# Float64 words turned into float32 through a PSUM bank, in a fused attention and two-layer expert kernel

## The chip, the cores and the metric

One NeuronCore of a Trainium2 chip (trn2) runs the whole program in one launch. The metric is the device time of one execution in microseconds (us), from the first to the last instruction and what lies around them; the median of three runs stands for the kernel.

## The reference, cut to what matters

Three layers follow each other on 1536 tokens (2 sequences of 768) of 384 channels.

```python
def reference(...):
    # 1: linear attention with a decaying state, 8 heads of 48
    state = w * state + k_t v_t ;  y_t = r_t (state + (u * k_t) v_t)
    # 2: dense layer, d_ff = 2048
    h = x @ w_in
    g = np.maximum(h, 0.0) + alpha * np.minimum(h, 0.0)
    x = g @ w_out
    # 3: each token goes to one of 8 experts (argmax of x @ w_gate), at most 384 tokens each
    y = np.maximum(x @ w1[e], 0.0) @ w2[e]
    out = softmax weight of e * y
```

Two inputs, `w_in` (384x2048) and `w_out` (2048x384), come as float64 (a float32 draw times a double). The kernel reads them as pairs of 32-bit words and makes float32 out of them itself.

## The kernel before

The dense layer is computed in 3 blocks of 512 tokens (`SIZES`), each in 16 slices of 128 hidden units; slice g is unit group g % 16 of block g // 16. A slice (`moe1_slice`, L603) does, in the order in which its instructions stand in each engine's queue: the steps of `work[g][5]`; the first product on TensorE (L599, 9 matmuls of 512 columns, since each factor is split into a high and a low float32r part and three of the four products are taken); on ScalarE the leak (L615); `work[g][0]`; on VectorE the second half of the leak (L618); on ScalarE the high part `gh` (L619); `work[g][1]`; on VectorE the low part `gl` (L622); `work[g][2]` and `work[g][3]`; the second product of slice g-2 on TensorE (L584); `work[g][4]`. Every engine takes its queue in order, so a step that waits holds all that stands behind it on its engine. The first product of slice g writes one of two banks (`ps_h`), so it waits for `gl` of slice g-2.

The second product of a block (`moe1_second`, L575) has four accumulators of 128 tokens x 384 channels, one PSUM bank each (`ps_acc`, four banks): per slice 4 x 3 matmuls of 384 columns, with the activations as the stationary operand and `w_out` as the moving one.

Attention runs ahead of the dense layer: tiles 0 to 3 before slice 0, tiles 4 to 7 in the slices of block 0, tiles 8 to 11 in those of block 1, in steps that `PHASES` (L314) puts into the slots: `turn` (TensorE transposes L182, L194; then VectorE L188 writes `rT`, ScalarE L202 `kT`, GpSimd a bonus), `score0` (TensorE L209, VectorE L212 writes `A`), `score1`, `output` (TensorE L218, L225, L236; VectorE L228 and the state), `finish` (TensorE L261; ScalarE L269, VectorE L270). Their PSUM tiles come in turn from two banks (`ps_a`).

The weights of the dense layer come in 8 pieces (q = 0 to 7, two slices each), and each piece in two parts (0: of `w_in`, 1: of `w_out`) of 128x768 numbers. `convert_moe1` (L339) turns one part into float32 and splits it. With `f` a scratch tile in SBUF (`spare`), `low` and `high` the two words of each number, its steps are `m0` (ScalarE L355, f from high), `s0` (VectorE L358, on f alone), `s1` (VectorE L361, f from low and f), `s2` (VectorE L364, low from high and f) and `s3` (ScalarE L367 the high part, GpSimd L368 the low part, each 128x768). Two parts are done before slice 0 (q = 0 and 1, part 0); the other 14 are spread over block 0 by `CONVERT` (L993): a step's number p, counted from slice `at`, means slice p // 5 and slot (5, 0, 1, 2, 4)[p % 5]. The two parts of a piece have different scratch halves for q < 4.

After a block its four accumulators are copied to SBUF (`evac` in `routing_steps`, L423) as rows; each 128 rows are turned for the gate product (`logit`, L428, then `logit_mm`, L437); the rows are scattered to `disp` in DRAM by expert. The experts follow; ahead of them one early block of expert 0 is computed (`Early`), and `keep_warm` (L752) fills TensorE with 6 matmuls (`warm_e`) while the rows of expert 0 are read back.

Of the kernel before, what the change touches and what calls it, by code (L numbers as in the profile page):

```python
# [18 lines left out]
P = 128  # L19
# [4 lines left out]
def kernel(  # L24
# [16 lines left out]
    nc = tc.nc  # L41
# [6 lines left out]
    DC = DM // P  # L48
# [269 lines left out]
    def rows_of(blk):  # L318
        return p1.tile([P, max(SIZES), ROW], F32, tag="rows", name=f"rows{blk}")
# [9 lines left out]
    def load_moe1(q, parts=(0, 1)):  # L329
        if 0 in parts:  # L330
            t = wpool.tile([P, 4 * DC * EF], I32, tag="w", name=f"rm{q}")
            raws[q] = (t[:, 0:2 * DC * EF], t[:, 2 * DC * EF:])
            nc.sync.dma_start(raws[q][0].rearrange("p (c n) -> p c n", c=DC),
                              moe_w_in[:, q * EF:(q + 1) * EF].bitcast(I32).rearrange("(c p) n -> p c n", p=P))
        if 1 in parts:
            nc.sync.dma_start(raws[q][1].rearrange("p (c n) -> p c n", c=2),
                              moe_w_out[q * EF:(q + 1) * EF, :].bitcast(I32).rearrange("(c p) n -> p c n", p=P))

    def convert_moe1(q, part, eng):  # L339

        n = DC * EF
        raw = raws[q][part].rearrange("p (n t) -> p n t", t=2)
        if part == 0:
            wsl[q] = wpool.tile([P, 4 * n], F32R, tag="w", name=f"wm{q}")
            if q in LOAD_AT:
                load_moe1(LOAD_AT[q])
        hi = wsl[q][:, part * 2 * n:part * 2 * n + n]
        lo = wsl[q][:, part * 2 * n + n:part * 2 * n + 2 * n]
        low, high = raw[:, :, 0], raw[:, :, 1]
        at = part * n if 2 * q < 8 else 0  # L350
        f = spare[:, at:at + n].bitcast(I32)

        def m0():

            nc.scalar.activation(f.bitcast(F32), high.bitcast(F32), AF.Copy, scale=2.0 ** -112)  # L355

        def s0():
            nc.vector.tensor_scalar(f, f, 3, 0x7FFFFFF8, op0=ALU.logical_shift_left, op1=ALU.bitwise_and)  # L358

        def s1():  # L360
            nc.vector.scalar_tensor_tensor(f, low, 29, f, op0=ALU.logical_shift_right, op1=ALU.bitwise_or)  # L361

        def s2():
            nc.vector.scalar_tensor_tensor(low, high, -0x80000000, f, op0=ALU.bitwise_and, op1=ALU.bitwise_or)  # L364

        def s3():
            nc.scalar.copy(hi, low.bitcast(F32))  # L367
            eng.tensor_tensor(lo, low.bitcast(F32), hi.bitcast(F32), ALU.subtract)  # L368

        return [m0, lambda: None, s0, s1, s2, s3]  # L370
# [44 lines left out]
    def routing_steps(blk, R, s0, SUB, before=()):  # L415
# [4 lines left out]

        end = blk == NBLK - 1

        def evac(s):  # L423
            def f():
                nc.scalar.copy(R[:, s0 + s, 0:DM], accs[(blk, s0 + s)])
            return f

        def logit(s):  # L428
            pt = bank(f"px2_{nm}_{s}", "acc" if end else "att")
            for c in range(DC):  # L430
                nc.tensor.transpose(pt[:, c * P:(c + 1) * P], R[:, s0 + s, c * P:(c + 1) * P], ident)
            pool, tag = ((p1, "x2T"), (p2, "cv"), (p2, "cv"), (p1, "x2T"))[s0 + s if end else 0]
            T[s] = pool.tile([P, DC, P], F32, tag=tag, name=f"x2T{nm}_{s}")
            src = pt[:, 0:DM].rearrange("p (c t) -> p c t", c=DC)
            return lambda: (nc.vector.tensor_copy if end and s0 + s < 2 else nc.scalar.copy)(T[s], src)

        def logit_mm(s):  # L437
            if s == 0 and end:
                T["pl"] = bank(f"pl{nm}")
                T["lg"] = T["pl"][:, 0:SUB * E].rearrange("p (s e) -> p s e", s=SUB)  # L440
            elif s == 0:
                T["lg"] = p2.tile([P, SUB, E], F32, tag="lg", name=f"lg{nm}")
            pl = T["pl"][:, s * E:(s + 1) * E] if end else bank(f"pl{nm}_{s}")[:, 0:E]
            for c in range(DC):
                for x in range(2):
                    nc.tensor.matmul(pl[64 * x:64 * x + 64], T[s][:, c, 64 * x:64 * x + 64], wg[:, c, :],
                                     start=(c == 0), stop=(c == DC - 1), skip_group_check=True)
            return (lambda: None) if end else lambda: nc.vector.tensor_copy(T["lg"][:, s, :], pl)

# [102 lines left out]
        def pair(s):  # L552
            def f(now=True):
                then = []
                if s > 0:
                    then.append(logit_mm(s - 1))
                if s < SUB:
                    then.append(logit(s))
                if now:
                    for t in then:  # L560
                        t()
                return then
            return f

        T["logit"], T["logit_mm"] = logit, logit_mm
        ev = [evac(s) for s in range(SUB)]
        T.update(choose=choose, weigh=weigh, count=count, place=place, scatter=scatter, total=total)
        steps = [pair(s) for s in range(SUB + 1)] + [lambda: weave(choose()), settle]
        return ev, steps, T
# [285 lines left out]
    with tc.manual_schedule():  # L855
# [134 lines left out]
        c1[5]()  # L990


        CONVERT = {0: (0, 0, 0, 0, 2, 3), 1: (-5, 1, 1, 1, 5, 9), 2: (-4, -2, -1, 2, 3, 7), 4: (-1, 0, 2, 5, 6, 7), 5: (-4, -1, 0, 1, 4, 6), 3: (-4, 0, 2, 5, 5, 7), 6: (-3, -1, 2, 4, 5, 7), 7: (-6, -6, -4, -2, 2, 4)}  # L993
        OTHERS = (-1, -1, 0, 0, 0, 5)
        work = [([], [], [], [], [], []) for _ in range(NBLK * NFT)]
        for q in range(NW):
            for x in range(2):
                if (q, x) in ((0, 0), (1, 0)):
                    continue
                at = 2 * q - 3 if x == 0 else 2 * q  # L1000
                c = []

                def step(n, c=c, q=q, x=x):
                    if n == 0:
                        c.extend(convert_moe1(q, x, nc.gpsimd))
                    c[n]()
                for n, p in enumerate(CONVERT.get(at, OTHERS)):
                    g = at + p // 5
                    work[g][(5, 0, 1, 2, 4)[p % 5]].append(lambda n=n, step=step: step(n))
# [147 lines left out]
```

## Time and profile before

| | |
|---|---|
| median of 3 runs | 466.55 us (466.14 to 466.82) |
| profiled execution | 466.23 us, span 464.5 us |
| busy: TensorE matmul / VectorE / ScalarE / GpSimd | 437.4 / 271.0 / 208.2 / 157.7 us |
| mean granted TensorE clock | 0.989 of full speed |

The span runs from the first to the last instruction; 1.7 us lie around it. Busy shares are averages over the whole program, and block 0 (about 36 to 133 us), in which the weights are converted, looks different from the rest; so the views below cut the time into stretches.

### The profile page before, as it was taken

The numbers are of one execution on the slowest core, as the hardware profiler recorded it, in microseconds if no ns is written. First come the engines' busy times: TensorE is split into PE (matmuls) and PEld (weight loads), VectorE is DVE, ScalarE is ACT, GpSimd is POOL, SyncE is SP. The second block draws the span as 40 slices with busy tenths as digits, with TensorE's granted clock in tenths as the row PEclk, the third lists the DMA queues.
The fourth block names the chain that finished last, engine by engine and source line by source line (L and its number), as shares of the span: only waits on it lengthen the run. The fifth ranks groups of instructions, "written<-read, shape, count | busy, mean of one in ns | idle before, by whom it ended". The sixth has DMA issues, their size and how long they took to land. (4 is left out here: it accounts for less than half of the span.)

```text
span 464.5 us, 7861 instructions
## 1 busy us (share of the span) xinstructions
PE 437.4 (94%) x3039; PEld 385.1 (83%) x3039; DVE 271.0 (58%) x470; ACT 208.2 (45%) x344; POOL 157.7 (34%) x138
## 2 busy tenths in 40 slices
PE   7977799699899999999999999999999999999995
PEld 6766699588788988989988888987988889898884
DVE  6998998999753444445333665354463535452651
ACT  1236634354344333323244444336473646553761
POOL 6855457464440231100300030033343515241660
PEclk9999979989999999999999999999999999999999
DMA  6999950649610207101700020018956556580200
GB/s 129 229 281 250 318 157 4 183 158 361 172 30 15 52 2 233 57 0 43 299 1 1 0 87 0 1 56 290 382 178 239 188 169 212 172 271 35 72 10 25
DMA packets 70605, 62.28 MB, mean 134 GB/s; under 512 B 41935, under 2 KB 58239, under 8 KB 70561
## 3 DMA queue, kind: packets, MB, share of 16 engines
q1 hardware_dynamic: 68832, 57.29, 41.1%
q0 software_dynamic: 1728, 4.40, 2.5%
q8 instruction: 28, 0.46, 0.4%
q14 instruction: 17, 0.13, 0.1%
HBM read 49.99 MB, written 12.62 MB: 135 GB/s over the span
## 5 line engine op out<-in xcount | busy, mean ns | idle before, releaser
L584 PE MATMUL acc<-wm,gh 128*128 128x384 f32 x384 | 102.0, 347 | 0.5 <-POOL wm L368 0.5
L599 PE MATMUL h<-xh,wm 128*128 128x512 f32 (+1 forms) x294 | 86.2, 402 | 4.4 <-DVE gl L622 4.4
L618 DVE SCALAR_TENSOR_TENSOR h<-ng,sign,h 128x512 f32<-128x512 f32 x48 | 36.1, 752 | 68.2 <-ACT ng L615 68.2
L584 PEld LDWEIGHTS acc<-wm,gh 128*128 128x128 f32 x384 | 69.9, 191 | 4.7 <-POOL wm L368 0.8
L775 PE MATMUL eh<-we,d 128*128 128x512 f32 x252 | 65.1, 403 | 4.5 <-PEq L847 3.2
L584 PE MATMUL acc<-wm,gl 128*128 128x384 f32 x192 | 65.4, 341 | 0.0
L599 PEld LDWEIGHTS h<-xh,wm 128*128 128x128 f32 x294 | 52.6, 190 | 14.2 <-issue 2.8
L615 ACT ACTIVATE ng<-h,slope 128x512 f32<-128x512 f32 x48 | 33.1, 689 | 60.1 <-PE h L599 60.0
L775 PEld LDWEIGHTS eh<-we,d 128*128 128x128 f32 x252 | 45.7, 188 | 15.5 <-issue 4.4
L619 ACT CAST gh<-h 128x512 fp32r<-128x512 f32 x48 | 28.1, 586 | 60.8 <-DVE h L618 60.8
L674 ACT CAST we<-re 128x768 fp32r<-128x768 f32 x64 | 50.6, 839 | 9.6 <-DMA re<-in_moe_w_dram 6.8
L677 POOL TENSOR_TENSOR we<-re,we 128x768 fp32r<-128x768 f32 x21 | 40.6, 1932 | 38.5 <-ACT we L674 32.2
L790 DVE TENSOR_TENSOR hl<-pht,hh 128x512 fp32r<-128x512 f32 x28 | 19.4, 692 | 51.6 <-ACT hh L789 49.8
L368 POOL TENSOR_TENSOR wm<-rm,wm 128x768 fp32r<-128x768 f32 x16 | 32.2, 2013 | 47.4 <-ACT wm L367 43.6
L799 PE MATMUL ey<-we,hh 128*128 128x384 f32 x224 | 48.1, 346 | 0.0
L677 DVE TENSOR_TENSOR we<-re,we 128x768 fp32r<-128x768 f32 x43 | 40.3, 965 | 11.9 <-ACT we L674 8.9
L522 POOL DMA_INDIRECT disp<-rows,sl x12 | 12.6, 1051 | 99.9 <-DVE run L543 64.4
L599 PE MATMUL h<-xl,wm 128*128 128x512 f32 (+1 forms) x147 | 42.1, 395 | 0.1
L622 DVE TENSOR_TENSOR gl<-h,gh 128x512 fp32r<-128x512 f32 x48 | 33.0, 687 | 15.6 <-ACT gh L619 15.6
L799 PEld LDWEIGHTS ey<-we,hh 128*128 128x128 f32 x224 | 37.8, 189 | 0.3 <-ACT hh L789 0.3
L584 PEld LDWEIGHTS acc<-wm,gl 128*128 128x128 f32 x192 | 36.6, 191 | 0.0
L599 PEld LDWEIGHTS h<-xl,wm 128*128 128x128 f32 x147 | 27.7, 191 | 7.0 <-DVE xl L270 0.3
(181 smaller groups left out, 618.8 us busy)
## 6 DMA issues: line engine op xcount, KB each, us to landing
re<-in_moe_w_dram SPq DMA_DIRECT2D x32, 768.0 KB, 7.2
rm<-in_moe_w_in_dram SPq DMA_DIRECT2D x8, 768.0 KB, 8.1
rm<-in_moe_w_out_dram SPq DMA_DIRECT2D x8, 768.0 KB, 7.5
disp<-rowss SPq DMA_DIRECT2D x1, 4825.0 KB, 16.0
drow<-disp SPq DMA_DIRECT2D x7, 579.0 KB, 3.9
out_dram<-rowss SPq DMA_DIRECT2D x1, 2304.0 KB, 22.4
kn<-in_k_dram SPq DMA_DIRECT2D x10, 192.0 KB, 4.6
rn<-in_r_dram SPq DMA_DIRECT2D x10, 192.0 KB, 4.8
```

Of the source, the lines that this page charges most:

```text
L368: eng.tensor_tensor(lo, low.bitcast(F32), hi.bitcast(F32), ALU.subtract)
L584: nc.tensor.matmul(accs[(blk, s)], gs[g][a][:, s * P:(s + 1) * P], wout[b][:, ft % 2, :], start=(ft == 0 and n == 0), stop=(ft == NFT - 1 ...
L599: nc.tensor.matmul(phs[g][:, cols[0]:cols[1]], win[a][:, c, o:o + P], xs[b][:, c, cols[0]:cols[1]], start=(n == 0), stop=(n == 3 * DC - 1))
L615: nc.scalar.activation(ng, ph, AF.Relu, scale=slope[:, ft:ft + 1])
L618: nc.vector.scalar_tensor_tensor(ph, ng, sign[:, ft:ft + 1], ph, op0=ALU.mult, op1=ALU.add)
L619: nc.scalar.copy(gh, ph)
L622: nc.vector.tensor_tensor(gl, ph, gh.bitcast(F32), ALU.subtract)
L674: nc.scalar.copy(t[:, sl], src[:, sl])
L677: le.tensor_tensor(t[:, sl2], src[:, sl], t[:, sl].bitcast(F32), ALU.subtract)
L775: nc.tensor.matmul(ph[q], d[x][:, c, :], ww[y][:, c, :], start=(n == 0), stop=(n == 3 * DC - 1))
L790: nc.vector.tensor_tensor(hl, pt, hh.bitcast(F32), ALU.subtract)
L799: nc.tensor.matmul(py, hT[q][x][:, c * P:(c + 1) * P], ww[y][:, c, :], start=(q == 0 and not low and c == 0 and y == 0), stop=(q == 1 and ...
```

## The change

- In block 0 (`TURNED`) the second product is summed transposed: the weights are the stationary operand, the activations the moving one, in three accumulators of 128 channels x 512 tokens, so 3 x 3 matmuls of 512 columns per slice. Its results are copied to an SBUF tile `x2T` (three ScalarE copies of 512 columns for four of 384), which feeds the gate product directly; what is turned by TensorE now is the other direction, from `x2T` to rows (`turn_back` in the place of `logit`).
- The fourth accumulator bank is the scratch `f` of the conversion for all but the two parts done before slice 0. Both parts of a piece (q from 2) are converted as one run of 1536 numbers in three chunks of 512; part 1 of pieces 0 and 1 in two chunks of 384. A chunk is `m0` on ScalarE and `s0`, `s1`, `s2` together on VectorE; there is one `f`, so a chunk's `m0` waits for the chunk before. `s3` stays 128x768.
- The positions of the steps in the slots are new (`CONVERT`).
- `warm_e` becomes 8 matmuls of 256 columns in plain float32 with a stationary operand of 32 columns, in the four column groups of the array in turn.

```diff
+    TURNED = (0,)
...
+            raws[(q, "all")] = t
...
-        raw = raws[q][part].rearrange("p (n t) -> p n t", t=2)
+        raw = raws[q][0 if part is None else part].rearrange("p (n t) -> p n t", t=2)
+        if part is None:
+            raw = raws[(q, "all")].rearrange("p (n t) -> p n t", t=2)
...
-        at = part * n if 2 * q < 8 else 0
-        f = spare[:, at:at + n].bitcast(I32)
...
+        if part == 0:
+            f, w = spare[:, 0:n].bitcast(I32), n
+        else:
+            if "f" not in late:
+                late["f"] = bank("f", "acc").bitcast(I32)
+            f, w = late["f"], n // 2 if part == 1 else 512
+
+        def m0(o):
+
+            nc.scalar.activation(f[:, 0:w].bitcast(F32), high[:, o:o + w].bitcast(F32), AF.Copy, scale=2.0 ** -112)
+
+        def s0(o):
+            nc.vector.tensor_scalar(f[:, 0:w], f[:, 0:w], 3, 0x7FFFFFF8, op0=ALU.logical_shift_left, op1=ALU.bitwise_and)
+
+        def s1(o):
+            nc.vector.scalar_tensor_tensor(f[:, 0:w], low[:, o:o + w], 29, f[:, 0:w],
+                                           op0=ALU.logical_shift_right, op1=ALU.bitwise_or)
+
+        def s2(o):
+            nc.vector.scalar_tensor_tensor(low[:, o:o + w], high[:, o:o + w], -0x80000000, f[:, 0:w],
+                                           op0=ALU.bitwise_and, op1=ALU.bitwise_or)
...
+        steps = []
+        for o in range(0, n if part else 2 * n, w):
+            steps += [lambda o=o: m0(o), lambda o=o: (s0(o), s1(o), s2(o))]
+            if part is None and o + w > n > o:
+                steps.append(lambda: s3(0))
+        return steps + [lambda: s3(1)]
...
+                if turned:
+                    nc.scalar.copy(x2T[blk][:, s], accs[(blk, s)])
+                else:
+                    nc.scalar.copy(R[:, s0 + s, 0:DM], accs[(blk, s0 + s)])
...
+        def turn_back(s):
+            pt = bank(f"pR{nm}_{s}")
+            for c in range(DC):
+                nc.tensor.transpose(pt[:, c * P:(c + 1) * P], x2T[blk][:, c, s * P:(s + 1) * P], ident)
+            return lambda: nc.scalar.copy(R[:, s, 0:DM], pt[:, 0:DM])
...
+                for c in range(DC):
+                    if ft == 0:
+                        accs[(blk, c)] = bank(f"acc{blk}_{c}", "acc")
+                    for n, (a, b) in enumerate(PASS):
+                        nc.tensor.matmul(accs[(blk, c)], wout[b][:, ft % 2, c * P:(c + 1) * P], gs[g][a],
+                                         start=(ft == 0 and n == 0), stop=(ft == NFT - 1 and n == 2))
...
-        CONVERT = {0: (0, 0, 0, 0, 2, 3), 1: (-5, 1, 1, 1, 5, 9), 2: (-4, -2, -1, 2, 3, 7), 4: (-1, 0, 2, 5, 6, 7), 5: (-4, -1, 0, 1, 4, 6), 3: (-4, 0, 2, 5, 5, 7), 6: (-3, -1, 2, 4, 5, 7), 7: (-6, -6, -4, -2, 2, 4)}
-        OTHERS = (-1, -1, 0, 0, 0, 5)
+        CONVERT = {0: (0, 0, 1, 2, 3), 1: (11, 12, 13, 14, 15), 2: (3, 4, 6, 7, 8, 8, 9, 13), 3: (16, 17, 18, 19, 20, 21, 22, 23)}
+        for q, a in ((4, 5), (5, 7), (6, 9), (7, 12)):
+            CONVERT[q] = [5 * a + x for x in (-2, -1, 1, 2, 3, 3, 4, 8)]
...
+        for q in (0, 2, 1, 3, 4, 5, 6, 7):
+            c = []
+
+            def step(n, c=c, q=q):
+                if n == 0:
+                    c.extend(convert_moe1(q, 1 if q < 2 else None, nc.gpsimd))
+                c[n]()
...
+                    t = wpool.tile([P, 4 * DC * EF], F32, tag="w", name=f"x2T_{blk}")[:, 0:DC * BLK]
+                    x2T[blk] = t.rearrange("p (c t) -> p c t", c=DC)
...
-        keep_warm("warm_e", "h", 6, early.d[0][:, 0, :], exp_w(0, 0)[0][:, 0, :])
+        warm = bank("warm_e", "h")
+        for _ in range(2):
+            for j in range(4):
+                nc.tensor.matmul(warm[32 * j:32 * j + 32, 0:2 * P], early.rows[:, 0, 0:32], raws[("e", 0, 0)][:, 0:2 * P],
+                                 start=True, stop=True, skip_group_check=True)
```

## Rows read from the trace of the kernel before

**Rows 1.** The page: TensorE busy tenths, 40 slices of 11.6 us each.
```profile
PE   7977799699899999999999999999999999999995
```
**Rows 2.** Stretches: PE, PEld, DVE, ACT, POOL busy; granted clock; DMA share, GB/s.
```profile
36.00:57.01 21.01, 16.24 (x94) 13.19 (x91) 19.49 (x26) 12.42 (x20) 10.25 (x7) 1.00 1.04 280
57.01:101.30 44.29, 40.05 (x315) 35.07 (x316) 42.21 (x48) 19.50 (x32) 28.30 (x20) 0.88 0.40 112
101.30:131.20 29.90, 28.31 (x196) 24.64 (x195) 25.51 (x31) 15.26 (x25) 10.75 (x6) 1.00 0.78 251
131.20:300.00 168.80, 168.80 (x1172) 150.62 (x1171) 77.23 (x160) 63.55 (x111) 24.84 (x24) 1.00 0.17 56
```
**Rows 3.** TensorE in order of time: start, us, work, idle before and its releaser.
```profile
57.06 1.22 PE L218 MATMUL py<-S,rT 128*128 128x96 f32 x8 [1.66 <-DVE rT L188]
...
92.57 0.90 PE L261 MATMUL px<-ident,cv 128*128 128x128 f32 x3 [3.52 <-DVE A L212]
```
**Rows 4.** One 1 us stretch after the first of these gaps, columns as in Rows 2.
```profile
58.00:59.00 1.00, 1.00 (x17) 0.83 (x17) 1.00 (x1) 0.16 (x1) 1.00 (x2) 0.50 1.06 381
```
**Rows 5.** VectorE and GpSimd in order of time: a conversion beside GpSimd, and one alone.
```profile
115.67 0.96 DVE L361 SCALAR_TENSOR_TENSOR rowss<-rm,rowss 128x768 int32<-128x768 int32 x1
115.68 2.68 POOL L368 TENSOR_TENSOR wm<-rm,wm 128x768 fp32r<-128x768 f32 x1 [3.78 <-DVE rowss L358]
116.67 2.51 DVE L364 SCALAR_TENSOR_TENSOR rm<-rm,rowss 128x768 int32<-128x768 int32 x1
...
124.95 0.55 DVE L358 TENSOR_SCALAR rowss<-rowss 128x768 int32<-128x768 int32 x1
...
126.53 0.96 DVE L364 SCALAR_TENSOR_TENSOR rm<-rm,rowss 128x768 int32<-128x768 int32 x1
```
**Rows 6.** VectorE busy on L358, then L361, then L364 alone, by stretch.
```profile
36.00:57.01 21.01, 4.26 (x4) 1.00 1.04 280
57.01:101.30 44.29, 5.96 (x6) 0.88 0.40 112
...
36.00:57.01 21.01, 3.64 (x4) 1.00 1.04 280
57.01:101.30 44.29, 11.85 (x7) 0.88 0.40 112
...
36.00:57.01 21.01, 3.64 (x3) 1.00 1.04 280
57.01:101.30 44.29, 10.46 (x7) 0.88 0.40 112
```
**Rows 7.** VectorE groups that read PSUM, 30 to 330 us: busy, mean ns, idle before.
```profile
L618 DVE SCALAR_TENSOR_TENSOR h<-ng,sign,h 128x512 f32<-128x512 f32 x48 | 36.1, 752 | 68.2 <-ACT ng L615 68.2
L622 DVE TENSOR_TENSOR gl<-h,gh 128x512 fp32r<-128x512 f32 x48 | 33.0, 687 | 15.6 <-ACT gh L619 15.6
```
**Rows 8.** ScalarE groups, 30 to 330 us, columns as in Rows 7.
```profile
L619 ACT CAST gh<-h 128x512 fp32r<-128x512 f32 x48 | 28.1, 586 | 60.8 <-DVE h L618 60.8
...
L367 ACT CAST wm<-rm 128x768 fp32r<-128x768 f32 x15 | 13.5, 898 | 2.0 <-DVE rm L364 2.0
...
L250 ACT COPY S<-Sc 64x192 f32<-64x192 f32 x14 | 4.9, 351 | 5.0 <-DVE Sc L248 4.8
```
**Rows 9.** TensorE in order of time: a slice of block 0, undisturbed.
```profile
133.28 0.86 PE L599 MATMUL h<-xh,wm 128*128 128x512 f32 x3
...
135.38 0.51 PE L584 MATMUL acc<-wm,gh 128*128 128x384 f32 x2
...
137.47 0.60 PE L182 MATMUL pr<-ident,rn 128*128 128x128 f32 x4
```
**Rows 10.** TensorE in order of time: two column groups; `warm_e` and what follows it.
```profile
78.81 1.14 PE L225 MATMUL py<-v,A 128*64 128x48 f32 x32
...
314.14 1.56 PE L756 MATMUL warm_e<-we,drow_f 128*128 128x512 f32 x6
...
316.02 1.04 PE L658 MATMUL pd<-ident,drow 128*128 128x128 f32 x6 [0.32 <-DMA drow<-disp]
```

More of the change, by code (lines that the diff above doesn't have):

```diff
@@ L341, in convert_moe1 @@
         n = DC * EF
-        raw = raws[q][part].rearrange("p (n t) -> p n t", t=2)
-        if part == 0:
+        raw = raws[q][0 if part is None else part].rearrange("p (n t) -> p n t", t=2)
+        if part is None:
+            raw = raws[(q, "all")].rearrange("p (n t) -> p n t", t=2)
+        if part != 1:
             wsl[q] = wpool.tile([P, 4 * n], F32R, tag="w", name=f"wm{q}")
@@ L346, in convert_moe1 @@
                 load_moe1(LOAD_AT[q])
-        hi = wsl[q][:, part * 2 * n:part * 2 * n + n]
-        lo = wsl[q][:, part * 2 * n + n:part * 2 * n + 2 * n]
         low, high = raw[:, :, 0], raw[:, :, 1]
-        at = part * n if 2 * q < 8 else 0
-        f = spare[:, at:at + n].bitcast(I32)
[L353 to L370, printed above, removed]
+        if part == 0:
[4 more added lines that the diff above has]
+            f, w = late["f"], n // 2 if part == 1 else 512
@@ new lines, in s3 @@
+        def s3(x):
+            hi = wsl[q][:, x * 2 * n:x * 2 * n + n]
+            lo = wsl[q][:, x * 2 * n + n:x * 2 * n + 2 * n]
+            src = low[:, x * n:(x + 1) * n] if part is None else low
+            nc.scalar.copy(hi, src.bitcast(F32))
+            eng.tensor_tensor(lo, src.bitcast(F32), hi.bitcast(F32), ALU.subtract)
+        if part == 0:
+            return [lambda: m0(0), lambda: None, lambda: s0(0), lambda: s1(0), lambda: s2(0), lambda: s3(0)]
+        steps = []
[3 more added lines that the diff above has]
+                steps.append(lambda: s3(0))
@@ L421, in routing_steps @@
         end = blk == NBLK - 1
+        turned = blk in TURNED
         def evac(s):
             def f():
-                nc.scalar.copy(R[:, s0 + s, 0:DM], accs[(blk, s0 + s)])
-            return f
+                if turned:
+                    nc.scalar.copy(x2T[blk][:, s], accs[(blk, s)])
+                else:
+                    nc.scalar.copy(R[:, s0 + s, 0:DM], accs[(blk, s0 + s)])
+            return f
+        def turn_back(s):
[3 more added lines that the diff above has]
+            return lambda: nc.scalar.copy(R[:, s, 0:DM], pt[:, 0:DM])
         def logit(s):
@@ L445, in logit_mm @@
                 for x in range(2):
-                    nc.tensor.matmul(pl[64 * x:64 * x + 64], T[s][:, c, 64 * x:64 * x + 64], wg[:, c, :],
+                    xs = x2T[blk][:, c, s * P:(s + 1) * P] if turned else T[s][:, c]
+                    nc.tensor.matmul(pl[64 * x:64 * x + 64], xs[:, 64 * x:64 * x + 64], wg[:, c, :],
                                      start=(c == 0), stop=(c == DC - 1), skip_group_check=True)
@@ L557, in f @@
                 if s < SUB:
-                    then.append(logit(s))
+                    then.append((turn_back if turned else logit)(s))
                 if now:
@@ L565, in routing_steps @@
         T["logit"], T["logit_mm"] = logit, logit_mm
-        ev = [evac(s) for s in range(SUB)]
+        ev = [evac(s) for s in range(DC if turned else SUB)]
         T.update(choose=choose, weigh=weigh, count=count, place=place, scatter=scatter, total=total)
@@ L573 @@
     gs = {}
+    x2T = {}
     def moe1_second(fts, subs=None):
         blk = fts[0] // NFT
+        if blk in TURNED:
+            for g in fts:
+                ft = g % NFT
+                wout = moe1_w(ft // 2)[1]
+                for c in range(DC):
[4 more added lines that the diff above has]
+                                         start=(ft == 0 and n == 0), stop=(ft == NFT - 1 and n == 2))
+            return
         for s in range(SIZES[blk]) if subs is None else subs:
@@ L990 @@
         c1[5]()
-        CONVERT = {0: (0, 0, 0, 0, 2, 3), 1: (-5, 1, 1, 1, 5, 9), 2: (-4, -2, -1, 2, 3, 7), 4: (-1, 0, 2, 5, 6, 7), 5: (-4, -1, 0, 1, 4, 6), 3: (-4, 0, 2, 5, 5, 7), 6: (-3, -1, 2, 4, 5, 7), 7: (-6, -6, -4, -2, 2, 4)}
-        OTHERS = (-1, -1, 0, 0, 0, 5)
+        CONVERT = {0: (0, 0, 1, 2, 3), 1: (11, 12, 13, 14, 15), 2: (3, 4, 6, 7, 8, 8, 9, 13), 3: (16, 17, 18, 19, 20, 21, 22, 23)}
+        for q, a in ((4, 5), (5, 7), (6, 9), (7, 12)):
+            CONVERT[q] = [5 * a + x for x in (-2, -1, 1, 2, 3, 3, 4, 8)]
         work = [([], [], [], [], [], []) for _ in range(NBLK * NFT)]
[L996 to L1009, printed above, removed]
+        for q in (0, 2, 1, 3, 4, 5, 6, 7):
[4 more added lines that the diff above has]
+                c[n]()
+            for n, p in enumerate(CONVERT[q]):
+                work[p // 5][(5, 0, 1, 2, 4)[p % 5]].append(lambda n=n, step=step: step(n))
         work[0][4].append(t3.state_up)
@@ L1047, in evac @@
             def evac(blk=blk):
+                if blk in TURNED:
+                    t = wpool.tile([P, 4 * DC * EF], F32, tag="w", name=f"x2T_{blk}")[:, 0:DC * BLK]
+                    x2T[blk] = t.rearrange("p (c t) -> p c t", c=DC)
                 ev, rt, _ = routing_steps(blk, rows_of(blk), 0, SIZES[blk])
```

## The prediction

> **What bounds the kernel now.** First the page's slices: TensorE is near full from about 105 us on and has its holes before that [rows 1]. Then the stretches: from 131 to 300 us TensorE never idles, so whatever block 0 ends later or earlier moves all that follows by as much; before that it loses time in three stretches, 21.01 - 16.24 = 4.8 us to 57, 44.29 - 40.05 = 4.2 us to 101, and 29.90 - 28.31 = 1.6 us to 131 [rows 2]. In the first two, VectorE is the full one: 19.49 of 21.01 and 42.21 of 44.29 us [rows 2]. Third, TensorE in order of time names what it waits for: VectorE's `rT` for 1.66 us at 57 and VectorE's `A` for 3.52 us up to 92.57 [rows 3]. The first of these is followed by a stretch at a granted clock of 0.50, which is the lower of the two levels, 1.2 GHz [rows 4]; over 57 to 101 the mean is 0.88, so some (1 - 0.88) x 44.29 = 5.3 us more went there [rows 2]. So up to slice 10 (101.3 us) VectorE's queue sets the pace, behind it TensorE's.
>
> What VectorE does there: the three conversion steps take 4.26 + 3.64 + 3.64 = 11.5 us up to 57 and 5.96 + 11.85 + 10.46 = 28.3 us from there to 101 [rows 6]; the rest of its queue is 19.49 - 11.5 = 8.0 and 42.21 - 28.3 = 13.9 us. Order of time shows why a step costs so different times: alone, L358 takes 0.55 and L364 0.96 us; beside GpSimd's L368 the same L364 takes 2.51 us and ends when GpSimd is through, and L368, started behind L361, takes 2.68 us [rows 5]. They exclude each other.
>
> **Part by part. The steps in PSUM.** With `f` in PSUM, `s1` and `s2` have one SBUF input each and `s0` none. L618 and L622, which read PSUM and at most one SBUF tensor, have means of 752 and 687 ns over 48 instances, a third of them in the stretch of the conversions, which leaves no room for stretches like L364's [rows 7]. So I take the stretching as gone. The price at 512 columns: L622's 0.69 for each (L618's 0.75 is the upper bound for all three; the lower is that `s0` keeps the rate of L358, 0.55 for 768, so some 0.45 here) [rows 5, 7]. Three in a chain with 0.03 us between them (L361 ends at 116.63, L364 starts at 116.67 [rows 5]): 2.13 us a chunk, bounds 1.9 to 2.3. Of 384 columns 0.13 to 0.14 us less a step, by the slope from L622's 512 to L364's 768 (0.27 us for 256 [rows 5, 7]): 1.71. On both sides of the change VectorE's conversion work is then: 2 x 2 x 1.71 + 18 x 2.13 = 45.2 us for the whole block, where the traced steps up to 101 alone took 39.8. The same work per piece is 3 x 2.13 = 6.4 against 2 x (0.55 + 0.96 + 0.96) = 4.9 if undisturbed [rows 5]: the chunks cost more than a lone conversion, and less than the stretched one, (39.8/10) x 2 = 8.0 for ten parts up to slice 10.
>
> Here two rules of the Trainium skill stand against each other. The first is what the rows show: SBUF — State Buffer, section Who interferes with whom, says that a VectorE instruction with two SBUF inputs contends with GpSimd's reads and one with at most one does not. The second speaks against the change: VectorE: DVE Perf Modes, section Why PSUM operands drop a tier, says that a PSUM operand takes from a single-source step its double rate. The trace bears it out as far as it goes, 0.55 us for 768 in SBUF [rows 5] against 0.69 for 512 in PSUM [rows 7]; by the first rule alone a piece would be 4.9 us, by both it is 6.4.
>
> **Where the chunks stand.** This is the larger term. Up to `rT` of tile 5 (end of turn(5), for which TensorE waits at 57.06 [rows 3]) the old order has 11.5 us of conversion in VectorE's queue. The new positions put before it both parts of 384 (4 chunks: positions 0 and 2, 12 and 14), all three chunks of piece 2 (4, 7, 9) and the first two of piece 3 (17, 19): 4 x 1.71 + 5 x 2.13 = 17.5 us. With the other 8.0 us that is 25.5 us from about 36.3, so 61.8 at the earliest. Four waits come on top, since ScalarE takes its queue in order and there is one `f`: after `gl` of slice 0 the next `m0` stands behind a high part (0.90 [rows 8]) that itself waits for the chunk before, 0.9 us; the leak of slice 1 stands behind two copies of the state (2 x 0.35) and `kT` (a 128x512 copy like L619, 0.59), which wait for VectorE behind a chunk, 1.3 us; the third chunk of piece 2 again behind a high part, 0.9; the leak of slice 3 behind the high part of piece 1 and itself 0.69, 1.6 [rows 8]. That makes 61.8 + 4.7 = 66.5, say 67, against 57: TensorE gets `rT` 10 us later, and sits through 7 to 8 us of it in one piece.
>
> After that the new order has less: ten chunks, 21.3 us, up to slice 10 against 28.3. VectorE needs 21.3 + 13.9 = 35.2, so 102 if it never waits. TensorE needs 44.29 - 4.2 - 5.3 = 34.8 at full clock, so 101.8 if it never waits. Both bounds are where the old kernel is (101.3), but the two take turns: walking the queues in program order, TensorE still waits for `A` of tile 5 (2.7), `rT` of tile 6 (2.2) and the output of tile 6 (0.8), and slice 10 begins at 106, 5 late. I take the walk, since the same walk with the old order and the old durations meets the traced starts of slices 2 to 15 within 1 us but for one; its end comes 1.0 late, which I take off. Behind slice 10 the old order loses 1.6 us [rows 2] with 4 of 14 parts still to convert; the new one has one piece left and waits 0.3, and `gl` comes in time: -2.3 with the walk. So +5 - 2.3 - 1.0 = +1.7. The clock: 1.66 us of idle brought 0.50 [rows 3, 4], so 7 us will; half of that falls where VectorE is late anyway: +0.3 to +3, I take +1.3. Sum +3.0.
>
> **The second product transposed.** Nine matmuls of 512 columns (L599) take 135.38 - 133.28 = 2.10 us, twelve of 384 (L584) 137.47 - 135.38 = 2.09 [rows 9]: 4608 columns either way. Nothing, on both sides 0.1 us in a slice.
>
> **Evacuation and the gate.** Three copies for four, the same number of transposes and copies to turn back; in block 1, where TensorE is full and ScalarE is not (63.55 of 168.8 us [rows 2]). Nothing; if that cover were gone, the copies would cost some 0.5 us each, L619's 0.59 being the bound [rows 8]. `x2T` takes one of the two buffers that are free after the conversion and gives it back in block 1.
>
> **`warm_e`.** It runs 314.14 to 315.70, and then TensorE waits 0.32 us for the rows from DRAM [rows 10]: room for 1.88 us. Plain float32 at 256 columns isn't in the trace; L225, plain float32 in two column groups, does 32 instructions in 1.14 us [rows 10], 36 ns for 48 columns each. With 16 instructions of 256 columns at that rate in pairs it would be 3.0 us, with all four groups at once half of it, 1.5. So 0 to +1.2; I take 0, since the next work is the DMA's, and keep +1.2 for the range.
>
> **Sum.** 466.23 for the profiled execution + 3.0 = 469.2; the median of the runs lies 0.3 higher, so 469.5 us.
>
> **The rivals.** (1) *VectorE catches up and TensorE is fed*: chunks of 1.9 us (the lower bound) or ScalarE ahead of its queue. Each 0.1 us of a chunk moves the end by 1.8 us, as 18 chunks stand in line; at 1.9 what is won behind slice 10 outweighs the late `rT`, and the end is 466.5 + 3.0 - 4.1 = 465.4, down to 464 without the clock's loss. From about 1.9 us it decides for faster. For it: VectorE's conversions fall from 39.8 for ten parts, so some 54 for fourteen, to 45 us. Against it: 0.69 and 0.75 are the rows at this shape. A chunk at the undisturbed rate of the old steps, 4.9/3 = 1.65 us, would give 461; no row shows a PSUM step at that rate, and I give it 0.03 of this rival's chance. (It is what the Trainium skill's first rule above gives without the second.) (2) *The gain and the late start cancel*, within 0.2% (0.9 us): chunks near 1.95, 466.5. (3) *TensorE's gap costs the clock twice*, at 59 and again at 77 to 90, where it would wait 2 to 3 us each; with `warm_e` serial as well: 3.0 + 2 + 1.2, so 472 to 474. (4) *The change doesn't free VectorE from GpSimd*: if `s1` and `s2` still waited for it, a third of L364's stretch (1.55 us [rows 5]) over 18 chunks is 9 us: 478.
>
> **How the numbers follow.** Forecast (+1.3 to +6) 0.50; rival 1 0.24; rival 2 0.14; rival 3 0.08; rival 4 0.04. The forecast's own range is 467.8 to 472.5. For 8 in 10 the range reaches down into rival 1, to 463.8, and up to rival 3, to 473.5. 0.2% is about what a measurement of this kernel can tell from no change. Faster: rival 1, 0.24. Same: rival 2, 0.14. Slower: 0.50 + 0.08 + 0.04 = 0.62.
>
> **What would show it.** L358, L361 and L364's successors at 0.69 us each with a narrow spread, beside GpSimd or not (else rival 4); `rT` of tile 5 near 67 and a TensorE gap of 7 us before it, with a clock of 0.50 behind it; slice 10 near 106; from slice 11 no wait for VectorE; block 0's second products at 2.1 us a slice; `warm_e` under 1.9 us. I am wrong if ScalarE's `m0` into PSUM or VectorE's steps are much shorter than 0.6 and 0.69, or if TensorE reaches slice 10 before 102.

## The result and the profile after

The changed kernel takes 470.18 us (median of 4 runs, 469.01 to 470.31) against 466.69 us of the kernel before beside it: a ratio of 1.0069, 95% interval 1.0049 to 1.0090. It is slower by 0.7%, 3.5 us; 469.5 was forecast. The profiled execution, from which the views below are, took 469.01 us with a span of 467.3 against 464.5.

Lines have moved: L355, L358, L361 and L364 (`m0`, `s0`, `s1`, `s2`) are now L361, L364, L367 and L371; the high and the low part, L367 and L368, are L378 and L379; L584, L599, L615, L618 and L622 are L617 (transposed) or L627, L642, L658, L661 and L665. The recurrence is one to three lines further down (`kT` L203, `pa` L210, `A` L213, `py` L219).

The page's slices answer to [rows 1]: of the slices of 11.7 us the fourth and the sixth are half empty now, and TensorE's clock is low in the fifth to the seventh.

```profile
PE   7975959999999999999999999999999999999995
PEclk9999778999999999999999999999999999999999
```

The stretches answer to [rows 2], with bounds moved to the gaps of this kernel (columns as there: length; PE, PEld, DVE, ACT, POOL busy; granted clock; DMA share, GB/s).

```profile
36.00:57.01 21.01, 15.40 (x69) 12.16 (x70) 16.53 (x27) 10.92 (x20) 8.98 (x7) 0.84 1.02 274
57.01:65.90 8.89, 4.07 (x21) 2.90 (x19) 7.21 (x13) 4.14 (x7) 4.07 (x3) 0.89 0.08 30
65.90:106.36 40.46, 38.78 (x295) 31.32 (x296) 35.52 (x58) 20.32 (x34) 18.83 (x15) 0.90 0.44 113
106.36:133.50 27.14, 27.14 (x179) 22.16 (x177) 19.78 (x32) 14.09 (x24) 13.86 (x12) 1.00 0.86 284
```

Up to slice 10, which begins at 106.56 us, TensorE idles 5.6 + 4.8 + 1.7 = 12.1 us, where it idled 9.0 up to 101.3 [rows 2]; behind it not at all, where it had idled 1.6. VectorE, full in both early stretches before, now has 4.5 of 21.01 us free in the first. In order of time (start, us, work, idle before and its releaser), the waits that answer to [rows 3]:

```profile
41.51 0.94 PE L642 MATMUL h<-xh,wm 128*128 128x512 f32 x3 [2.10 <-DVE gl L665]
47.35 2.08 PE L210 MATMUL pa<-rT,kT 64*128 64x128 f32 x16 [3.51 <-ACT kT L203]
65.90 2.02 PE L219 MATMUL py<-S,rT 128*128 128x96 f32 x8 [4.82 <-ACT kT L203]
81.24 0.55 PE L262 MATMUL px<-ident,cv 128*128 128x128 f32 x3 [1.16 <-DVE A L213]
```

The two long ones end on a copy of ScalarE's. The second ends on the copy of tile 5's `kT`, with `rT` of that tile still to come:

```profile
65.27 0.58 ACT L203 COPY kT<-pk 128x512 f32<-128x512 f32 x1
67.71 0.68 DVE L189 TENSOR_TENSOR rT<-pr,tabE 128x512 f32<-128x512 f32 x1
```

What ScalarE, VectorE and GpSimd did before the first of them:

```profile
41.59 0.63 ACT L361 ACTIVATE f<-rm 128x512 f32<-128x512 f32 x1
41.76 1.87 POOL L379 TENSOR_TENSOR wm<-rm,wm 128x768 fp32r<-128x768 f32 x1 [3.59 <-ACT wm L378]
42.25 0.70 DVE L364 TENSOR_SCALAR f<-f 128x512 int32<-128x512 int32 x1 [0.88 <-ACT f L361]
42.98 0.69 DVE L367 SCALAR_TENSOR_TENSOR f<-rm,f 128x512 int32<-128x512 int32 x1
43.71 0.69 DVE L371 SCALAR_TENSOR_TENSOR rm<-rm,f 128x512 int32<-128x512 int32 x1
44.31 0.35 DVE L248 TENSOR_TENSOR Sc<-pg,Sc 128x192 f32<-128x192 f32 x1
44.70 1.17 DVE L249 TENSOR_TENSOR Sc<-Sc,w 128x192 f32<-128x192 f32 x1
45.96 0.73 ACT L251 COPY S<-Sc 64x192 f32<-64x192 f32 x2 [3.75 <-DVE Sc L249]
46.71 0.59 ACT L203 COPY kT<-pk 128x512 f32<-128x512 f32 x1
```

VectorE waits for ScalarE's `m0`, then does a whole chunk; behind it stand the two steps of the state (0.35 and 1.17 us; the second takes 0.36 at 72.96); ScalarE's queue, whose next work is a copy of that state, stands still for 3.75 us, and `kT`, whose input TensorE had made at 37 us, stands behind that. In the kernel before the same copy waited 0.42 us:

```profile
42.15 0.73 ACT L250 COPY S<-Sc 64x192 f32<-64x192 f32 x2 [0.42 <-DVE Sc L248]
```

This is how one wait arises: each chunk is cheap, and its first two steps are not drawn out beside GpSimd's low part at 41.76, but it stands in two in-order queues ahead of what TensorE needs.

The conversion's groups (busy us, mean ns, idle before), to be held against [rows 5, 7]:

```profile
L367 DVE SCALAR_TENSOR_TENSOR f<-rm,f 128x512 int32<-128x512 int32 x18 | 12.5, 696 | 0.6
L364 DVE TENSOR_SCALAR f<-f 128x512 int32<-128x512 int32 x18 | 12.5, 695 | 6.9 <-ACT f L361 6.9
L371 DVE SCALAR_TENSOR_TENSOR rm<-rm,f 128x512 int32<-128x512 int32 x18 | 12.4, 689 | 0.6
```

### The profile page after: what moved, and what is told of

It reads as the page before. It is cut to its first block, busy times and chain, and to the rows that moved or that the text cites. A ratio compares the mean times of both kernels' runs of the same rounds, so it can differ in the third digit from the quotient of the medians.

```text
span 467.3 us, 7829 instructions
## 1 busy us (share of the span) xinstructions
PE 438.0 (94%) x3001; PEld 378.7 (81%) x3001; DVE 262.7 (56%) x494; ACT 209.7 (45%) x351; POOL 150.4 (32%) x138
## 5 line engine op out<-in xcount | busy, mean ns | idle before, releaser
L642 PE MATMUL h<-xh,wm 128*128 128x512 f32 (+1 forms) x294 | 85.6, 400 | 2.1 <-DVE gl L665 2.1
L661 DVE SCALAR_TENSOR_TENSOR h<-ng,sign,h 128x512 f32<-128x512 f32 x48 | 36.2, 754 | 73.6 <-ACT ng L658 73.6
L627 PE MATMUL acc<-wm,gh 128*128 128x384 f32 x256 | 66.7, 342 | 0.0
L642 PEld LDWEIGHTS h<-xh,wm 128*128 128x128 f32 x294 | 52.6, 189 | 12.2 <-issue 2.5
L658 ACT ACTIVATE ng<-h,slope 128x512 f32<-128x512 f32 x48 | 33.0, 687 | 63.7 <-PE h L642 63.6
L627 PEld LDWEIGHTS acc<-wm,gh 128*128 128x128 f32 x256 | 46.0, 188 | 2.5
L379 POOL TENSOR_TENSOR wm<-rm,wm 128x768 fp32r<-128x768 f32 x16 | 29.9, 1868 | 43.0 <-ACT wm L378 43.0
L627 PE MATMUL acc<-wm,gl 128*128 128x384 f32 x128 | 43.2, 338 | 0.0
L642 PE MATMUL h<-xl,wm 128*128 128x512 f32 (+1 forms) x147 | 41.7, 391 | 0.5 <-DVE xl L271 0.5
L665 DVE TENSOR_TENSOR gl<-h,gh 128x512 fp32r<-128x512 f32 x48 | 32.9, 686 | 14.8 <-ACT gh L662 14.1
L617 PE MATMUL acc<-gh,wm 128*128 128x512 f32 x96 | 33.7, 434 | 0.0
L642 PEld LDWEIGHTS h<-xl,wm 128*128 128x128 f32 x147 | 27.3, 188 | 7.2 <-DVE xl L271 0.7
```

Of the source, the lines that this page charges most:

```text
L379: eng.tensor_tensor(lo, src.bitcast(F32), hi.bitcast(F32), ALU.subtract)
L617: nc.tensor.matmul(accs[(blk, c)], wout[b][:, ft % 2, c * P:(c + 1) * P], gs[g][a], start=(ft == 0 and n == 0), stop=(ft == NFT - 1 and n ...
L642: nc.tensor.matmul(phs[g][:, cols[0]:cols[1]], win[a][:, c, o:o + P], xs[b][:, c, cols[0]:cols[1]], start=(n == 0), stop=(n == 3 * DC - 1))
L658: nc.scalar.activation(ng, ph, AF.Relu, scale=slope[:, ft:ft + 1])
L661: nc.vector.scalar_tensor_tensor(ph, ng, sign[:, ft:ft + 1], ph, op0=ALU.mult, op1=ALU.add)
L665: nc.vector.tensor_tensor(gl, ph, gh.bitcast(F32), ALU.subtract)
```

## The experiments

Two questions: what the PSUM bank is worth, and whether the loss lies in the chunks' price or in where they stand. Theory A: the bank frees VectorE, and the positions in the in-order queues lose more than that. Theory B: the bank is worth little, or 18 chunks are too much for VectorE wherever they stand. A position p in `CONVERT` is slice p // 5 and a place in it; the list of a piece (from 2 on) is `m0`, steps, `m0`, steps, split 0, `m0`, steps, split 1, where a split is the high and the low part (`s3`).

**Without the bank (e1).**

```diff
-                late["f"] = bank("f", "acc").bitcast(I32)
+                late["f"] = spare[:, 0:512].bitcast(I32)
```

> The changed kernel with the scratch f of 512 columns in SBUF instead of the PSUM bank; positions, chunks and the transposed sum stay. Theory A (the PSUM scratch frees VectorE from GpSimd, the loss is all in the positions): the stretching comes back, steps beside GpSimd's 1.87 us take up to 2.5 us, block 0 ends 10 to 18 us later, 480 to 488 us. Theory B (what the change loses is the PSUM operand's price, since s0 loses its double rate): s0 falls from 0.70 to about 0.42 us, 18 chunks win 18 x 0.28 = 5 us of VectorE, 465 to 468 us. If neither matters: 470.

Measured: 483.63 us, ratio 1.0365 (1.0348 to 1.0382). The three steps take 979, 969 and 931 ns on average instead of 695, 696 and 689: 0.80 us more a chunk, times 18 is 14.4 us, and 483.6 - 470.2 = 13.5 us was measured. For chunks of 512 with one `f` the bank is worth that at these positions; B falls in its first form.

**Splits later, chunks where they were (e2).**

```diff
+        CONVERT = {0: (0, 0, 1, 2, 4), 1: (11, 12, 13, 14, 22), 2: (3, 4, 6, 7, 15, 8, 9, 21),
+                   3: (16, 17, 18, 19, 23, 21, 22, 38), 4: (23, 24, 26, 27, 38, 28, 29, 38),
...
```

> The changed kernel with every chunk where it is, and only the splitting steps s3 (ScalarE's high part, GpSimd's low part) put later, behind the leak of the slice in whose way they stood. Theory A (positions; the waits of ScalarE's queue in front of the leak are part of the loss): the four waits of 0.9 to 1.6 us in front of the leak and of m0 shrink, slice 10 begins near 101.5 instead of 106.6, about 465 us. Theory B (the price of the PSUM steps sets VectorE's pace): VectorE's work is the same, so 469 to 470.

Measured: 478.17 us, ratio 1.0259 (1.0228 to 1.0291). Neither theory: the splits came so late that TensorE waited for them, 3.62 us in one piece for a low part in slice 8, and in slice 14 2.75 us for a high and 1.30 for a low part.

**Chunks and splits later (e3, and e4 with `f` in SBUF).**

```diff
+        CONVERT = {0: (0, 0, 1, 2, 4), 1: (11, 12, 15, 17, 22), 2: (4, 6, 6, 7, 15, 9, 10, 21),
+                   3: (18, 21, 21, 22, 23, 22, 26, 38), 4: (26, 28, 31, 32, 38, 33, 37, 38),
...
```

> The changed kernel with the same chunks, their order and their work, but chunks and splitting steps spread later over the slices, so that fewer chunks stand before rT of tile 5 and A of tile 5. Theory A (positions): TensorE's waits of 3.5 us before slice 3 and 4.8 us before tile 5's state go, the clock stays at its upper level, slice 10 begins near 93 and slice 15 near 118.5, so 13 us earlier: 456 to 459 us, below both kernels. Theory B (price of the PSUM steps): VectorE has the same 45 us of steps, 468 to 470.

> As the run with all positions moved, and f of 512 columns in SBUF. Theory A: with GpSimd in the way again 12 to 16 us later than that run with f in PSUM, 469 to 474 us, so that without the PSUM bank even good positions give no gain over the kernel before. Theory B: s0 at its double rate, the same as or up to 5 us faster than the run with f in PSUM.

Measured: 471.14 us, ratio 1.0107 (1.0055 to 1.0158), and with `f` in SBUF 477.88 us, 1.0231 (1.0214 to 1.0248). The waits for `kT` went, to none and 1.06 us, but others took their place in e3:

```profile
58.59 1.13 PE L219 MATMUL py<-S,rT 128*128 128x96 f32 x8 [1.06 <-ACT kT L203]
63.20 0.51 PE L617 MATMUL acc<-gh,wm 128*128 128x512 f32 x1 [1.94 <-ACT wm L378]
65.14 0.79 PE L617 MATMUL acc<-gh,wm 128*128 128x512 f32 x1 [1.43 <-POOL wm L379]
...
126.35 0.96 PE L642 MATMUL h<-xh,wm 128*128 128x512 f32 x3 [2.22 <-ACT wm L378]
```

So these two runs didn't decide between A and B: a split has a deadline, the first matmul that reads it, and it was missed. Between them the bank is worth 6.7 us, half of what it was, perhaps because part of what SBUF costs falls into those waits.

**Chunks later, each split right behind its chunk (e5); and positions by a walk of the four queues (e8).** The chunks of e5 are those of e3 but for piece 7. The walk takes every instruction in program order with its measured duration; both keep each split ahead of its first reader.

```diff
+        CONVERT = {0: (0, 0, 1, 2, 3), 1: (11, 12, 15, 17, 18), 2: (4, 6, 6, 7, 8, 9, 10, 14),
+                   3: (18, 21, 21, 22, 23, 22, 26, 30), 4: (26, 28, 31, 32, 33, 33, 37, 38),
...
```

> The changed kernel with other positions for the chunks: spread later over slices 2 to 14 so that fewer stand before the transposed rT, kT and A of tiles 5 and 6, but every high/low split stays right behind the chunk that it needs (e3 had them late as well, and TensorE waited for them). Same PSUM steps, same second product. Theory A (the positions in the in-order queues set the time, not the price of the steps): slice 10 begins at 95 to 99 us instead of 106.6, TensorE waits under 3 us in one piece before it, and the time is 459 to 464 us, faster than both kernels. Theory B (18 chunks of 2.1 us are too much for VectorE's queue wherever they stand): 468 to 472 us. Rival C (the granted clock falls to the lower level after each short gap, whatever its size): 464 to 467 us with the waits gone.

```diff
+        CONVERT = {0: (0, 1, 1, 2, 5), 1: (12, 13, 16, 17, 18), 2: (2, 5, 6, 7, 16, 11, 12, 13),
+                   3: (17, 19, 20, 20, 22, 21, 22, 31), 4: (22, 25, 28, 29, 35, 32, 35, 40),
+                   5: (36, 37, 39, 39, 42, 45, 45, 54), 6: (47, 48, 50, 51, 56, 53, 55, 57),
+                   7: (56, 57, 60, 62, 64, 62, 63, 66)}
```

> The changed kernel with positions found by a walk of the four queues with the measured durations (chunk 2.14 us, high part 0.90, low part 1.87), each split only as late as its first reader allows. Theory A: slice 10 begins at 94 to 98 us, the time is 455 to 461 us, and 2 to 5 us below e5. Theory B: 468 to 472 us. If the walk leaves out a wait as it did in e3 (there 3 us were missing), 460 to 464 us.

Measured: 461.47 us, ratio 0.9880 (0.9847 to 0.9913), and 458.87 us, 0.9815 (0.9788 to 0.9841). The second beats both kernels, by 8.0 us (466.91 beside it) and 11.3. Its stretches, at the bounds of [rows 2]:

```profile
36.00:57.01 21.01, 17.07 (x89) 12.68 (x89) 19.46 (x34) 12.61 (x22) 10.39 (x7) 1.00 1.06 271
57.01:101.30 44.29, 41.21 (x324) 33.32 (x323) 41.59 (x68) 24.91 (x42) 22.86 (x20) 1.00 0.55 166
101.30:131.20 29.90, 29.90 (x193) 24.43 (x192) 20.91 (x32) 15.19 (x25) 13.36 (x9) 1.00 0.64 192
```

and the same copy of the state, two lines of ScalarE's queue that answer to those at 45.96 and 46.71 above:

```profile
42.18 0.73 ACT L251 COPY S<-Sc 64x192 f32<-64x192 f32 x2 [0.68 <-DVE Sc L249]
42.93 0.59 ACT L203 COPY kT<-pk 128x512 f32<-128x512 f32 x1
```

The steps are the same (means of 693, 696 and 689 ns) and as many, VectorE is full again, and the wait of 3.75 us is 0.68. Theory A holds, B falls in its second form as well: it was the order, not the load. Rival C falls by e5, which ends below its range and keeps a clock of 1.00 behind waits of 2.09 and 1.51 us.

Not all of what e8 wins is shorter waits. Up to slice 10 TensorE idles 59.52 - 52.51 = 7.0 us, where the changed kernel idled 70.56 - 58.45 = 12.1; the other 58.45 - 52.51 = 5.9 of the 11.0 us by which slice 10 starts earlier are matmuls, as many within one, at a clock of 1.00 instead of 0.88:

```profile
36.00:106.56 70.56, 58.45 (x387) 46.58 (x387) 59.41 (x96) 35.57 (x60) 31.89 (x23) 0.88 0.56 150
...
36.00:95.52 59.52, 52.51 (x386) 41.32 (x387) 55.79 (x92) 34.24 (x58) 32.41 (x26) 1.00 0.68 184
```

This split is that of the two profiled executions; the other runs have no stretches by which it could be made.

**Other positions by the same walk (e9)**, with the last splits later still.

```diff
+        CONVERT = {...
+                   6: (46, 48, 48, 48, 52, 51, 52, 60), 7: (55, 55, 56, 62, 62, 76, 77, 80)}
```

> Other spread positions by the same walk (0.9 us better than e8's in the walk, the last splits up to slice 16). If the time goes by the walk: 457 to 459 us, as e8 or just below. Rival (splits as late as this again hold TensorE, as in e3): 460 us or more.

Measured: 461.27 us (458.61 to 463.01), ratio 0.9860 (0.9825 to 0.9896). TensorE waits 1.42 us for the last low part at 130.94, the rival's mechanism in small, but that is not what the profile loses: from 36 to 140 us TensorE idles 104.00 - 97.71 = 6.3 us, less than e8's 104.00 - 96.99 = 7.0, at a mean clock of 0.93 against 1.00. Of the three falls of the clock, at 42, 60 and 131 us, only the last comes behind that wait. The profiled run took 463.01 us, another of the four 458.61, as e8's; whether these positions are worse than e8's stays open.

**The good positions without the bank (e10)**: the edit of e1 on that of e8.

> e8's positions with f in SBUF instead of a PSUM bank: nothing else differs from e8. Theory A2 (the bank and the positions are both needed: SBUF steps with two SBUF inputs stand behind GpSimd's low parts, and no order of the queue makes room for that): the walk gives 20 us more than e8, so 474 to 481 us. Theory A3 (with good positions the price of the steps is hidden, the bank is worth little): 459 to 464 us.

Measured: 474.81 us, ratio 1.0173 (1.0155 to 1.0191), so 15.9 us over e8: A2, for chunks of 512 with one `f`. The kernel before has its conversion in SBUF too, in another form (steps of 768, two scratch halves for q < 4), and takes 466.91; what that form would give at positions from the same walk was not run. So what the bank is worth against SBUF at its best isn't shown. The steps in order of time show the price and the mechanism at once, beside GpSimd's low part and without it:

```profile
86.66 2.04 POOL L379 TENSOR_TENSOR wm<-rm,wm 128x768 fp32r<-128x768 f32 x1
87.02 2.23 DVE L367 SCALAR_TENSOR_TENSOR rowss<-rm,rowss 128x512 int32<-128x512 int32 x1
89.28 0.69 DVE L371 SCALAR_TENSOR_TENSOR rm<-rm,rowss 128x512 int32<-128x512 int32 x1
90.71 0.43 DVE L364 TENSOR_SCALAR rowss<-rowss 128x512 int32<-128x512 int32 x1
91.17 0.69 DVE L367 SCALAR_TENSOR_TENSOR rowss<-rm,rowss 128x512 int32<-128x512 int32 x1
```

**Halves of the good positions**: pieces 0 to 3 as in e8 and the others as in the change (e11), and the reverse (e12) (the rows of the two `CONVERT` above, joined).

> The changed kernel with e8's positions for pieces 0 to 3 alone (those before the transposed rT and kT of tile 5); pieces 4 to 7 where the change put them. Theory A by the walk: tile 5's wait shrinks from 4.8 to about 2 us, slice 10 begins 6.5 us earlier than in the changed kernel (at 100), the waits for A of tile 5 and rT of tile 6 stay; 463 to 465 us. Rival (the early wait is only handed on, VectorE being full up to slice 10): 468 to 470 us.

> The other half: e8's positions for pieces 4 to 7, pieces 0 to 3 where the change put them. Theory A by the walk: TensorE still waits about 5 us for kT of tile 5, then no more; slice 10 begins at 100; 462 to 465 us. Rival (the late rT of tile 5 carries the whole loss, as the prediction had it): 468 to 470 us.

Measured: 463.01 us, ratio 0.9920 (0.9903 to 0.9938), and 465.36 us, 0.9972 (0.9955 to 0.9989). The leak of slice 10 starts at 101.83 and 104.33 us, against 109.02 in the changed kernel and 97.97 in e8: 7.2 and 4.7 us won, together 11.9, where both at once win 11.1. The early pieces cost more, but neither half carries the loss alone; e12 ends 0.4 us above the range of theory A. The stretches up to slice 10 of e11, then of e12, to be held against the two above, tell how:

```profile
36.00:99.37 63.37, 56.12 (x382) 44.04 (x381) 58.69 (x96) 35.12 (x59) 31.38 (x23) 0.92 0.62 164
...
36.00:101.89 65.89, 56.09 (x383) 44.84 (x381) 56.73 (x92) 33.64 (x57) 32.31 (x26) 0.87 0.59 161
```

TensorE idles 7.25 us in e11, nearly e8's 7.0, and 9.8 in e12. So the early pieces alone win back almost all of the idle time, and what slice 10 of e11 still lacks, against 95.52 in e8, is 3.6 us of matmuls at a lower clock. All four runs of e11 are longer than those of e8 (461.94 us at least against 459.18 at most), so it is not the profiled execution alone that is behind. In the second half's run the wait for tile 5's `kT` stands as before, and nothing after it:

```profile
46.84 2.08 PE L210 MATMUL pa<-rT,kT 64*128 64x128 f32 x16 [2.83 <-ACT kT L203]
65.40 2.02 PE L219 MATMUL py<-S,rT 128*128 128x96 f32 x8 [4.83 <-ACT kT L203]
```

**The second product alone (e6)**, on the kernel before.

```diff
+                        accs[(blk, c)] = bank(f"acc{blk}_{c}", "acc")
+                    for n, (a, b) in enumerate(PASS):
+                        nc.tensor.matmul(accs[(blk, c)], wout[b][:, ft % 2, c * P:(c + 1) * P], gs[g][a], ...)
...
-                then.append(logit(s))
+                then.append((turn_back if turned else logit)(s))
```

> The kernel before with one part of the change alone: block 0's second product summed transposed in three banks and turned back in block 1; the conversion stays in SBUF at its old positions. The prediction's step (9 matmuls of 512 columns for 12 of 384 cost the same, the copies are hidden in block 1): within 0.5 us of the kernel before, 466.2 to 467.4 us, nine matmuls of a slice in 2.1 us. Rival (the transposed form costs TensorE or the turning back holds block 1): 468 us or more. Rival (fewer banks and weight loads help): 466 us or less.

Measured: 466.59 us against 466.91, ratio 0.9986 (0.9973 to 1.0000): nothing that can be told from no change. Its nine matmuls run from 135.90 to 138.00, 2.10 us, in the changed kernel from 83.75 to 85.85, as predicted.

**The old `warm_e` (e7)** in the changed kernel.

```diff
-        warm = bank("warm_e", "h")
...
+        keep_warm("warm_e", "h", 6, early.d[0][:, 0, :], exp_w(0, 0)[0][:, 0, :])
```

> The changed kernel with the old warm_e (the stretch of matmuls that keeps TensorE busy before the first expert). The prediction's step (hidden behind the wait for the rows from DRAM): 469.5 to 470.5 us, as the changed kernel. Rival (the new float32 form in four column groups takes longer and costs up to 1.2 us): 468.8 us or less.

Measured: 471.49 us, ratio 1.0076 (1.0051 to 1.0101); above the forecast range, but the interval holds the changed kernel's 1.0069. The new form is shorter, not longer: 1.07 us against 1.56. Little comes of it: from the start of the rows' read to the first matmul on them 2.66 us pass in the changed kernel (316.16 to 318.82), 2.99 with the old form (319.30 to 322.29). The rest of the 1.3 us between the medians isn't explained. First the changed kernel, then the one with the old form:

```profile
317.81 1.07 PE L1159 MATMUL warm_e<-re,drow_f 128*32 128x256 f32 x16
```

```profile
320.89 1.56 PE L799 MATMUL warm_e<-we,drow_f 128*128 128x512 f32 x6
```

The runs on the bank in one view (us, medians):

| positions | `f` in PSUM | `f` in SBUF | the bank's worth |
|---|---|---|---|
| of the change | 470.18 | 483.63 | 13.5 |
| splits too late (e3, e4) | 471.14 | 477.88 | 6.7 |
| by the walk (e8, e10) | 458.87 | 474.81 | 15.9 |

## Why the prediction was right, and where it was not

The forecast, +3.0 us by a late start and a gain behind it, came true: slice 10 at 106.56 (forecast 106), slice 15 at 132.11 against 128.97, +3.1. Point by point:

- **The price of a step.** 0.69 to 0.70 us for each of the three, as taken from [rows 7], and not stretched beside GpSimd, so rival 4 falls. The longest of all 54 took 0.70 us. The slope, 1.8 us for 0.1 us of a chunk, would make 14.4 us of e1's 0.80; 13.5 was measured.
- **The two rules.** Both rules of the Trainium skill that were weighed are seen in the runs. By SBUF — State Buffer, section Who interferes with whom, a VectorE step with at most one SBUF input is free of GpSimd, but only outside the two-port modes, an exception that the prediction left out. The same `s1` takes 2.23 or 0.69 us in SBUF and 0.70 in PSUM, and `s0`, with a single input, is drawn out in SBUF as well, 0.98 us on average in e1 against 0.43 alone; [rows 6] had it too, 4.26 us for four, where one alone takes 0.55. By VectorE: DVE Perf Modes, section Why PSUM operands drop a tier, `s0` loses its double rate, and it goes from 0.43 us in SBUF to 0.695; the prediction's rows for this were of L622, a step with two inputs, and only the runs with `f` in SBUF show it. The second costs 18 x 0.27 = 4.8 us of VectorE's time; the first is the larger.
- **A reading of [rows 5] was off.** L364 ends at 119.18, 0.82 us behind GpSimd's 118.36 and not with it; alone it takes 0.96. Nothing in the sum hangs on it.
- **The late `rT`.** It begins at 67.71, forecast near 67. Before it VectorE spent 5.72 + 5.73 + 5.59 = 17.0 us on conversion steps (17.5 forecast), 25.48 - 17.04 = 8.4 on the rest (8.0), and idled 31.41 - 25.48 = 5.9 (4.7 of waits, and the gaps between the steps).
- **The gap before tile 5's state: wrong.** Forecast were 7 to 8 us in one piece; it was 4.82. What `py` reads of tile 4 had long been there; by its releaser it waited for a buffer that `kT`'s copy freed at 65.85, while `rT` came at 68.39. And the waits that the forecast put behind it, for `A` 2.7, `rT` 2.2 and the output 0.8, measured 1.16, none and 0.5.
- **The missing wait: the mis-sized term.** The same mechanism had struck before, at `kT` of tile 4: 3.51 us of TensorE's time that the prediction doesn't name. It had the case, ScalarE's leak behind two copies of the state that wait for VectorE behind a chunk, at 1.3 us; ScalarE's wait there was 3.75 us against 0.42. It asked what this did to VectorE's queue, not what `kT` behind it did to TensorE. Too little here and too much later cancel: 12.1 - 9.0 = 3.1 us more idle. That the chunks make a late start was right; that these errors cancel in the sum is luck.
- **The clock.** It fell to 0.50 twice, at 47 to 53.7 and at 64 to 74.2 us, as rival 3 had it, though at other places. TensorE was busy for 6.4 and 8.3 us of that, half of which is 7.3; before it was 6.8 and 2.9, half 4.9 [rows 4 for the first]. So +2.4 us; +1.3 was taken, of 0.3 to 3. That a gap such as the 1.66 us before `py` brings 0.50 is not fixed either: in e11 a wait of 1.66 us before the same `py` was followed by the fall, in e8 one of 1.66 us was not. With the idle time, 3.1 + 2.4 = 5.5, that is slice 10's delay: 106.56 - 101.30 = 5.3.
- **Behind slice 10.** No wait up to 133.5, -1.6; slice 15 has won 2.1 in all, forecast -2.3. The rest, 0.5, wasn't followed up.
- **Second product, evacuation, `warm_e`.** Nothing to be seen in e6; some 0.3 us in favour of the new `warm_e` by the profile of e7, nothing sure by its time. Both prices of `warm_e`, 1.5 and 3.0 us, were too dear: its 16 instructions took 1.07 us.
- **Rival 1's condition: too narrow.** It asked for chunks of 1.9 us or less, or for ScalarE ahead of its queue, and priced only the first. e8 feeds TensorE with chunks of 2.1 us: 11.3 us below the changed kernel with the same instructions. The prediction took the positions as given and VectorE's load as the bound, 102 us for slice 10 if it never waits; slice 10 of e8 at 95.52, 5.8 us ahead of the kernel before, shows that the load itself could be moved: e8 puts two of piece 6's three chunks behind the start of slice 10, the change none.

## What to carry to other kernels

A step that no longer fights another engine for SBUF may win nothing until the queue is laid out anew, as here: ask for each in-order queue what stands behind the new piece and who waits for that, in both directions (here VectorE's chunk held ScalarE's copy, and that held TensorE). A step that is cut in pieces has room on both sides, from its input to its first reader's deadline; use it, but count the last link of the chain, since splits a slice too late took back all that the chunks had won. Two copies of a kernel that differ in one buffer, at good and at bad positions, tell the worth of the buffer from that of the order.

## What was not expected of the hardware

e8 and e11 have the same instructions in the same order up to slice 4. In both TensorE waits for `gl` of slice 0 at 41 us, 2.11 and 2.08 us long; then the granted clock stays at 1.00 (2.4 GHz) in e8, and in e11 it falls to 0.50 (1.2 GHz). The wait, and the stretch from 43 us, of e8 and then of e11:

```profile
41.58 0.94 PE L642 MATMUL h<-xh,wm 128*128 128x512 f32 x3 [2.11 <-DVE gl L665]
...
43.00:44.00 1.00, 1.00 (x6) 0.54 (x7) 0.97 (x2) 0.97 (x2) 0.00 (x0) 1.00 1.05 351
```

```profile
40.90 0.94 PE L642 MATMUL h<-xh,wm 128*128 128x512 f32 x3 [2.08 <-DVE gl L665]
...
43.00:44.00 1.00, 1.00 (x5) 0.35 (x3) 0.97 (x2) 1.00 (x2) 0.14 (x1) 0.50 1.21 270
```

So with a wait of some two us the instructions up to there don't settle the clock, as far as one profiled execution of each can show: one loses it and another doesn't. e9 fell there too, and again at 60 us behind a wait of 0.86 us, and its runs lie 4.4 us apart, at mean clocks of 0.983 to 0.993; e8's lie 1.1 apart. What else tells the cases apart, the runs don't show. For this kernel it means that a wait of a us or two costs more than its length in some of the executions.
